# Landmark attention and two MLPs on one core: two PSUM tiles for attention's banks, SyncE in written order, and a new order of the casts in batch 0

## The chip, the cores and the metric

One core of one Trainium2 chip. The metric is the device time of one execution in microseconds; three runs of the kernel before gave 1353.11, 1353.55 and 1353.95, median 1353.55.

## The reference

All tensors are float32. Batch 8, 8 heads, 576 positions, head size 64, 32 landmarks.

```
A  = softmax(q k_lm^T)      # q_lm, k_lm: means over 18 neighbouring positions
Bm = softmax(q_lm k_lm^T)
C  = softmax(q_lm k^T)
Z  = Bm^T / (norms of Bm);  six times: Z = 2 Z - Z Bm Z
x  = A Z C v                              # 4608 tokens x 512
x  = elu(x w_in) w_out                    # 512 -> 2048 -> 512
out = max(x w1, x w2, x w3) w_out2        # 512 -> 768 -> 512
```

## The kernel before

The program has two phases. The first goes through 256 slots, 32 for each of 8 batches, and makes attention and the first MLP; the second makes the maxout MLP from a copy of x in DRAM. The change is in the first phase only, almost all of it in batch 0's slots.

**A slot** (loop at L1414) is one half of a batch's tokens (288) and one block of 128 of the 2048 hidden features. `h_mm` (L689) issues six matmuls into `ph` (PSUM, two buffers) and on ScalarE Relu and Exp into `eh` (SBUF, two buffers); `h_post` (L706) finishes elu on VectorE (the post, L708) and splits the result into a rounded part `gt`, a cast on ScalarE (L97), and the low rest of it, a subtraction on GpSimd or VectorE (L99). In batch 0 that split is made one slot late; `G_LOW` says in which slots VectorE makes the subtraction. `x_mm` (L718) issues twelve matmuls of the slot three back, from `gt` and `wo`, into `x`. In batch 0 the features go in two passes (slots 0 to 7 and 8 to 15 are the two halves of the tokens with the first 8 blocks, 16 to 31 the rest); at the end of each pass ScalarE and VectorE copy `x` out, or VectorE adds it to what an earlier pass left.

**Attention's output is never multiplied out.** `w_step` (L656) multiplies the small matrix `mt` of a batch with 512 columns of w_in, in a pair of PSUM banks, and splits the result into `wp`, the weights of `h_mm`: a cast on ScalarE (L665) and a subtraction on VectorE (L670), the latter issued late in the slot. `w_both(n)` is that for batch 0 and n = 1 to 3.

**Weights** w_in and w_out arrive as 64-bit words (512 KB an item, 32 items) and are narrowed to float32 on the chip. An item is fetched into a place that an earlier item has left (`fetch1`, L1266, twelve places at most), widened on ScalarE (L114; in the form `BITS` a second ScalarE instruction, L119, scales the low word, in the form `BITS_V` VectorE does so, L127), narrowed on VectorE (L136), and, for w_out, cast (L182, ScalarE) and subtracted (L187, GpSimd). Items 0 to 9 are widened in the front, the part ahead of slot 0; from item 10 on a slot widens one item at its start and narrows, casts and subtracts the ones before it at its end.

**Attention of the next batch** runs inside the slots: `SECOND_SLOTS` gives the slot of each step for batch 1, all behind the post of the slot before (`after_post`). Steps: `q0`..`k1` sum q and k over 18 positions on VectorE (L300); `c0`, `c1` score C (L323: per half a pair of banks, a maximum on VectorE, L351, and a copy on ScalarE, L358, for each); `e`, `t` transpose; `cv` multiplies with v; `bbt` and `n0` to `n5` are Newton's steps (L612: a matmul, a product on VectorE, L580, a copy on ScalarE, L631, an add on VectorE, L633); `a10` to `a31` are A's softmax (L426: maximum on VectorE, subtraction on GpSimd, L432; exp on ScalarE, L440); `m` copies `mt` (L653).

**PSUM for attention** is one tile `banks` of two banks; `att_ps` gives out one bank in turn, `att_pair` both. In batch 0's front the banks of the MLP are used instead (tiles `pc`, `pe`, `pn`, `pa`, `pw` and so on).

**Order.** TensorE and VectorE run in the order written, ScalarE too until slot 27. In the front a string, `ORDER`, sets the order of attention's steps (letters B, V, A), of narrowings (c) and of widenings (w). SyncE, which issues all DMAs, and GpSimd are ordered by the framework's planner, which lets a DMA go ahead of one written earlier. Each queue is in order once it is planned: an instruction that waits holds all behind it. The framework makes an instruction wait for the earlier ones on the tiles that it touches.

```
banks = ps_a.tile([P, 2, 512], F32, name="banks")
...
turn[0] ^= 1
return Bank(banks[:, turn[0]], turn[0])
```

Of the kernel before, what the change touches and what calls it, by code (L numbers as in the profile page):

```python
# [9 lines left out]
F32 = mybir.dt.float32  # L10
# [9 lines left out]
def landmark_attention_mlp_maxout_kernel(  # L20
# [13 lines left out]
    nc = tc.nc  # L34
# [16 lines left out]
    FPN = 512 // P  # L51
    LAG = 3

    FIXED_ACT = 27
    RA = 3

    AHEAD2 = 5
# [2 lines left out]

    NF = 12
    DEPTH = 12
    EARLY = {2: range(8, 22), 3: range(8, 26)}
    FRONT = 10
    BY_ACT = range(12, 17)
    PAIRS = "i0 i0 o0 i1 i1 o2 o4 o6 i2 i2 o8 i3 i3 o10 o12 o14".split()

    ORDER = "BBBBwwBBVBBVVVVwwBVVBAcwBAwBcAwBAAwBAAwBAwBAAWc"


    G_LOW = [[0, 1] * 8, [0, 1] * 8]
# [74 lines left out]
    class Conversions:  # L146
# [58 lines left out]

    manual = ExitStack()
    manual.enter_context(
        tc.manual_schedule(engines={mybir.EngineType.DVE, mybir.EngineType.Activation})
    )

    ident = const.tile([P, P], F32, name="ident")
# [22 lines left out]

    spare = [0]

    banks = ps_a.tile([P, 2, 512], F32, name="banks")
    turn, last = [0], [None, None]

    class Bank:  # L240
# [19 lines left out]
    def att_ps(b, name):  # L260

        if b == 0 and spare[0] >= 0:
            spare[0] += 1
            n = spare[0] % 6
            if n < 4:
                return Bank(ps_x.tile([P, 512], F32, tag=f"x{n}", name=name))
            return Bank(ps_h.tile([P, 512], F32, tag="h", name=name))
        turn[0] ^= 1
        return Bank(banks[:, turn[0]], turn[0])

    def att_pair(b, name):

        if b == 0 and spare[0] >= 0:
            return [att_ps(b, name) for _ in range(2)]
        return [Bank(banks[:, g], g) for g in range(2)]

    def load_qk(b, r, nm):

# [147 lines left out]
    def soft_a1(b, g):  # L426
        x = state["x", b, g]
        sh = [P, 2 * NB2, M]
        t = att.tile([P, 2 * NB2], F32, tag=f"t18{g}", name="t18")
        nc.vector.tensor_reduce(out=t, in_=x, op=ALU.max, axis=AX.X)  # L430
        eng = nc.gpsimd if b < 2 and SOFT_SUB[b][g] else nc.vector
        eng.tensor_tensor(  # L432
            out=x, in0=x, in1=t.unsqueeze(2).to_broadcast(sh), op=ALU.subtract
        )
        if b:
            soft_ax(b, g)

    def soft_ax(b, g):
# [173 lines left out]
    def newton(b, i):  # L612
        cur, nxt, rd = rrs[i % 2], rrs[(i + 1) % 2], state.pop(("rd", b))
        pvs = []
        for gs in groups(b):
            pt = att_ps(b, "pn")
            pv = pt[:, : 2 * P].rearrange("p (g c) -> p g c", g=2)
            for g in gs:
                pt.put(
                    nc.tensor.matmul,  # L620
                    pv[:, g],
                    rd[:, g].rearrange("p h m -> p (h m)"),
                    cur[:, g],
                    start=True,
                    stop=True,
                )
# [5 lines left out]
        for gs, sl, pv in pvs:
            nc.vector.tensor_tensor(  # L633
                out=nxt[:, sl, M : M + D],
                in0=pv[:, sl, M : M + D],
                in1=cur[:, sl, M : M + D],
                op=ALU.add,
            )
# [50 lines left out]
    def h_mm(b, half, f):  # L689
        n, ff = divmod(f, FPN)  # L690
        ph = ps_h.tile([P, 512], F32, tag="h", name="ph")
        for g in range(2):
            wt = state["wp", b, n, g]
            wh = wt[:, 0, ff * P : (ff + 1) * P]
            wl = wt[:, 1, ff * P : (ff + 1) * P]
            ah, al = state["ah", b, half][:, g], state["al", b, half][:, g]
            for j, (a, c) in enumerate(((wh, ah), (wh, al), (wl, ah))):
                nc.tensor.matmul(  # L698
                    ph[:, :HF], a, c, start=(g == 0 and j == 0), stop=(g == 1 and j == 2)
                )  # L700
        e = r_s.tile([P, HF], F32, tag="eh", name="eh", bufs=2)
        nc.scalar.activation(e, ph[:, :HF], AF.Relu, scale=-1.0)  # L702
        nc.scalar.activation(e, e, AF.Exp, scale=-1.0)  # L703
        hps[b, half, f] = (ph, e)

    def h_post(b, half, f):  # L706
        ph, e = hps.pop((b, half, f))
        state["post"] = nc.vector.scalar_tensor_tensor(  # L708
            out=e, in0=e, scalar=1.0, in1=ph[:, :HF], op0=ALU.subtract, op1=ALU.max
        )  # L710
        held.append(((b, half, f), e))
        while len(held) > (b == 0):
# [478 lines left out]
    def att_steps(b):  # L1191
# [172 lines left out]
    def after_post(stp):  # L1364


        def go():
            with tc.issue_after(state["post"].ins):
                stp()

        return go

    at(0, load_att, 1)
    at(2, load_v, 1)
    for b in range(1, B):
        t0 = (b - 1) * NSL
        if b > 1:
# [36 lines left out]
    for t, sl in enumerate(seq):  # L1414
        if t == 0:
            scalar.close()
            scalar = ExitStack()
            manual.enter_context(tc.manual_schedule(engines={mybir.EngineType.PE}))
            vector.enter_context(tc.manual_schedule(engines={mybir.EngineType.DVE}))
            scalar.enter_context(tc.manual_schedule(engines={mybir.EngineType.Activation}))  # L1420
        if t == FIXED_ACT:
            scalar.close()
        h_mm(*sl)
        if t < len(items):
            stage(conv.widen, FRONT + t, form(FRONT + t))
        late = [fn(*args) for fn, args in plan[t]]
        h_post(*sl)
        for fn in late:
# [143 lines left out]
```

## Time and profile before

| | us |
|---|---|
| median of three runs | 1353.55 |
| profiled execution | 1353.35 |
| its span, first to last instruction | 1351.1 |
| front, up to the first matmul of slot 0 | 41.8 |
| slots 0 to 27 | 108.9 |
| mean granted TensorE clock, share of full speed | 0.987 |

The span is what the trace covers; 2.25 us of the profiled execution lie outside it. Busy times of engines overlap and don't add up. A row of a timeline merges neighbouring instructions of one kind: start, time from its start to the last one's end, engine, line, operation, output and inputs, count, and in brackets the idle time of the engine just before and what ended it.

### The profile page before, as it was taken

Reading aid. Unit: us, or ns where it says so; the run is one execution under the profiler, and the core shown is the slowest. Engines: PE = TensorE matmul, PEld = TensorE weight load, DVE = VectorE, ACT = ScalarE, POOL = GpSimd, SP = SyncE. Lnnn points to the kernel's source line nnn. Section 1 sums busy time; section 2 is a strip of 40 time slices with the busy share of each in tenths; the row PEclk is TensorE's granted clock in tenths of the full one; section 3 lists DMA queues with packets and bytes.
Section 4 is the critical chain, followed back from the end, with each engine's and each line's share of the span. In section 5 each row is a group of like instructions: output and inputs, shape, how many; then the busy total and the mean of one; then the engine's idle time right before and its main releaser. Section 6 shows DMA issues by size and latency. Waiting matters only on the chain.

```text
span 1351.1 us, 28435 instructions
## 1 busy us (share of the span) xinstructions
PE 1300.8 (96%) x11144; PEld 1228.5 (91%) x11144; DVE 834.0 (62%) x1613; ACT 672.2 (50%) x1559; POOL 656.9 (49%) x675
## 2 busy tenths in 40 slices
PE   4688999999999999999999999999999999999998
PEld 2577889899898998998999999999999999999998
DVE  7876745546546546455464456776677667668873
ACT  4665555656656656656566652322223223236451
POOL 1423323534435425435356456666666666665443
PEclk8789999999999999999999999999999999999999
DMA  9644105214214232242116243221322132279872
GB/s 354 231 127 156 36 19 166 73 68 135 100 56 136 92 120 90 66 166 85 56 66 189 65 132 98 87 98 55 114 87 87 56 110 91 86 281 324 295 243 79
DMA packets 102374, 168.03 MB, mean 124 GB/s; under 512 B 5984, under 2 KB 57824, under 8 KB 102240
## 3 DMA queue, kind: packets, MB, share of 16 engines
q1 hardware_dynamic: 102240, 166.22, 36.3%
q8 instruction: 87, 1.43, 0.4%
q14 instruction: 47, 0.39, 0.1%
HBM read 107.22 MB, written 58.98 MB: 123 GB/s over the span
## 4 chain that ended last, share of the span: by engine, by line
PE 85%; ACT 1%; DVE 1%; issue 1%; POOL 1%; DMA 0%; SPq 0%; DVEq 0%; POOLq 0%; ACTq 0%
PE p L1087 30%; PE x L733 27%; PE ph L698 13%; PE p L1164 10%; PE banks L256 6%; DMA words<-in_moe_w_dram 0%; POOL gt L99 0%; ACT eh L703 0%; ACT eh L702 0%; ACT wp L665 0%; DVE wp L670 0%; DVE eh L708 0%; DVE kT L300 0%; ACT gt L97 0%; POOL al L99 0%
## 5 line engine op out<-in xcount | busy, mean ns | idle before, releaser
L733 PE MATMUL x<-gt,wo 128*128 128x288 f32 x3072 | 471.5, 303 | 4.3 <-DVE xo L757 2.0
L733 PEld LDWEIGHTS x<-gt,wo 128*128 128x128 f32 x3072 | 425.2, 190 | 47.0 <-issue 27.7
L1087 PE MATMUL p<-xo,w 128*128 128x256 f32 x3402 | 410.3, 283 | 1.0 <-DVE xo L761 1.0
L1087 PEld LDWEIGHTS p<-xo,w 128*128 128x128 f32 x3402 | 408.6, 191 | 2.8 <-ACT xo L903 1.5
L99 POOL TENSOR_TENSOR gt<-eh,gt 128x288 fp32r<-128x288 f32 x240 | 195.7, 817 | 356.7 <-ACT gt L97 306.2
L698 PE MATMUL ph<-ah,wp 128*128 128x288 f32 x1024 | 250.4, 299 | 3.3 <-DVE eh L708 2.4
L708 DVE SCALAR_TENSOR_TENSOR eh<-eh,ph 128x288 f32<-128x288 f32 x256 | 114.4, 447 | 163.9 <-ACT eh L703 120.3
L942 POOL TENSOR_TENSOR u<-s,v 128x512 f32<-128x512 f32 x99 | 132.4, 1337 | 145.7 <-DVE v L940 144.1
L698 PEld LDWEIGHTS ph<-ah,wp 128*128 128x128 f32 x1024 | 181.8, 192 | 8.5 <-DVE eh L708 4.0
L702 ACT ACTIVATE eh<-ph 128x288 f32<-128x288 f32 x256 | 105.0, 410 | 124.2 <-PE ph L698 92.7
L97 ACT CAST gt<-eh 128x288 fp32r<-128x288 f32 x256 | 110.0, 430 | 103.4 <-DVE eh L708 103.4
L931 ACT COPY s<-p 128x512 f32<-128x512 f32 x99 | 58.0, 586 | 199.4 <-PE p L1087 166.5
L698 PE MATMUL ph<-al,wp 128*128 128x288 f32 x512 | 153.3, 299 | 0.0
L1164 PE MATMUL p<-wo,ho 128*128 128x256 f32 x1134 | 133.2, 280 | 0.0
L1164 PEld LDWEIGHTS p<-wo,ho 128*128 128x128 f32 x1134 | 133.1, 188 | 0.0
L703 ACT ACTIVATE eh<-eh 128x288 f32<-128x288 f32 x256 | 114.1, 446 | 5.6
L955 DVE TENSOR_TENSOR t<-p,u 128x512 f32<-128x512 f32 x81 | 55.7, 688 | 72.1 <-POOL u L942 69.6
L698 PEld LDWEIGHTS ph<-al,wp 128*128 128x128 f32 x512 | 98.0, 191 | 0.0
L1154 DVE TENSOR_TENSOR ho<-hf,ho 128x768 fp32r<-128x768 f32 x54 | 73.4, 1387 | 13.8 <-ACT ho L1152 13.1
L1094 DVE TENSOR_TENSOR t<-t 128x1024 f32<-128x1024 f32 x54 | 70.7, 1308 | 6.4 <-POOL t L945 0.4
L945 POOL TENSOR_TENSOR t<-u,s 128x256 f32<-128x256 f32 x81 | 67.2, 829 | 5.4
L1152 ACT CAST ho<-hf 128x768 fp32r<-128x768 f32 x63 | 51.1, 836 | 36.5 <-DMA hf<-hs 17.3
(165 smaller groups left out, 1342.2 us busy)
## 6 DMA issues: line engine op xcount, KB each, us to landing
hf<-hs SPq DMA_DIRECT2D x63, 384.0 KB, 4.4
hs<-t SPq DMA_DIRECT2D x27, 512.0 KB, 3.0
xs<-xo SPq DMA_DIRECT2D x36, 288.0 KB, 4.2
hs<-s SPq DMA_DIRECT2D x27, 384.0 KB, 3.4
qT<-in_q_dram SPq DMA_DIRECT2D x16, 576.0 KB, 6.1
kT<-in_k_dram SPq DMA_DIRECT2D x16, 576.0 KB, 7.6
words<-in_moe_w_dram SPq DMA_DIRECT2D x9, 1024.0 KB, 5.6
xf<-xs SPq DMA_DIRECT2D x9, 1024.0 KB, 5.1
```

The lines of the kernel that those rows point to most:

```text
L97: nc.scalar.copy(hi, src)
L99: eng.tensor_tensor(out=lo, in0=src, in1=hi.bitcast(F32), op=ALU.subtract)
L256: ins = fn(*args, **kw)
L698: nc.tensor.matmul(ph[:, :HF], a, c, start=(g == 0 and j == 0), stop=(g == 1 and j == 2))
L702: nc.scalar.activation(e, ph[:, :HF], AF.Relu, scale=-1.0)
L703: nc.scalar.activation(e, e, AF.Exp, scale=-1.0)
L708: state["post"] = nc.vector.scalar_tensor_tensor(out=e, in0=e, scalar=1.0, in1=ph[:, :HF], op0=ALU.subtract, op1=ALU.max)
L733: nc.tensor.matmul(xacc[ec][:, :HF], a, gt[:, c], start=(first and j == 0), stop=(last and j == 2),)
L942: nc.gpsimd.tensor_tensor(out=u57, in0=s57, in1=v.unsqueeze(1).to_broadcast([P, 2, 256]), op=ALU.add)
L1087: nc.tensor.matmul(dst, l, r, start=(c == 0 and j == 0), stop=(c == 1 and j == 2))
L1154: eng.tensor_tensor(out=lo, in0=v, in1=hi.bitcast(F32), op=ALU.subtract)
L1164: nc.tensor.matmul(dst, l, r, start=(c == 0 and n == 0), stop=(c == NP - 1 and n == 2))
```

## The change

Seven things change. (1) `banks` becomes two tiles of one bank each. (2) SyncE joins the engines in written order, up to slot 14. With it the loads of batch 1's q and k are written in slots 1 and 2 and that of v in slot 5. (3) In batch 0 the cast of `gt` of slot t-1 follows Exp of slot t on ScalarE, and its subtraction stands ahead of the post of slot t; `G_LOW` is turned round. (4) Widening moves from the start to the end of a slot, and all stages of an item from 10 on stand a slot later. (5) `BY_ACT` is empty: items 12 to 16 take the form in which VectorE scales the low word. `EARLY` gives the places of `wp` for one item less. (6) For batch 1 the exp of A's softmax is a step of its own (`ax0`, `ax1`), a slot behind its subtraction at the earliest, the sums stand a slot later, and Newton's add is issued behind the post. (7) `w_both(1)` moves from slot 2 to 3, `w_both(3)` from 17 to 18.

```
-    FIXED_ACT = 27
+    FIXED_SP, FIXED_ACT = 14, 27
-    EARLY = {2: range(8, 22), 3: range(8, 26)}
+    EARLY = {2: range(8, 21), 3: range(8, 26)}
-    BY_ACT = range(12, 17)
+    BY_ACT = ()
-    G_LOW = [[0, 1] * 8, [0, 1] * 8]
+    G_LOW = [[1, 0] * 8, [1, 0] * 8]
...
-        tc.manual_schedule(engines={mybir.EngineType.DVE, mybir.EngineType.Activation})
+        tc.manual_schedule(
+            engines={mybir.EngineType.DVE, mybir.EngineType.Activation, mybir.EngineType.SP}
+        )
...
-    banks = ps_a.tile([P, 2, 512], F32, name="banks")
+    banks = [ps_a.tile([P, 512], F32, tag=f"bank{g}", name=f"bank{g}") for g in range(2)]
...
-        return Bank(banks[:, turn[0]], turn[0])
+        return Bank(banks[turn[0]], turn[0])
...
-        return [Bank(banks[:, g], g) for g in range(2)]
+        return [Bank(banks[g], g) for g in range(2)]
...
-        if b:
+        if b > 1:
             soft_ax(b, g)
...  newton: the adds become a function add
+        if b == 1:
+            return add
+        add()
...
         nc.scalar.activation(e, e, AF.Exp, scale=-1.0)
         hps[b, half, f] = (ph, e)
+        gt_cast()
 
     def h_post(b, half, f):
         ph, e = hps.pop((b, half, f))
+        gt_low()
...
         held.append(((b, half, f), e))
-        while len(held) > (b == 0):
-            key, e = held.pop(0)
-            gt = r_s.tile([P, 2, HF], F32R, tag="gt", name="gt", bufs=LAG + 1)
-            split(e, gt[:, 0], gt[:, 1], key[0] == 0 and G_LOW[key[1]][key[2]])
-            gts[key] = gt
+        if b:
+            gt_cast()
+            gt_low()
+
+    def gt_cast():
+
+        for key, e in held:
+            gts[key] = gt = r_s.tile([P, 2, HF], F32R, tag="gt", name="gt", bufs=LAG + 1)
+            nc.scalar.copy(gt[:, 0], e)
+
+    def gt_low():
+        for (b, half, f), e in held:
+            gt = gts[b, half, f]
+            eng = nc.vector if b == 0 and G_LOW[half][f] else nc.gpsimd
+            eng.tensor_tensor(
+                out=gt[:, 1], in0=e, in1=gt[:, 0].bitcast(F32), op=ALU.subtract
+            )
+        held.clear()
...
+        if b == 1:
+            first += [(f"ax{g}", lambda g=g: soft_ax(b, g)) for g in range(2)]
...  SECOND_SLOTS
-        q0=3, k0=4, q1=5, k1=6, ...
+        q0=4, k0=5, q1=6, k1=7, ...
-        a10=20, a11=21, a20=23, ...
+        a10=20, a11=21, ax0=21, ax1=22, a20=23, ...
...
-    at(0, load_att, 1)
-    at(2, load_v, 1)
+    for n, (g, nm) in enumerate(((0, "q"), (0, "k"), (1, "q"), (1, "k"))):
+        at(1 + n // 2, load_qk, 1, g, nm)
+    at(5, load_v, 1)
...
-        at(tw - (2 if n == 1 else 3), w_both, n)
+        at(tw - (1, 3, 2)[n - 1], w_both, n)
...
+        if t == FIXED_SP:
+            sync.close()
...
         h_mm(*sl)
-        if t < len(items):
-            stage(conv.widen, FRONT + t, form(FRONT + t))
...
-        if t < len(items):
-            stage(conv.narrow, FRONT + t - 1, form(FRONT + t - 1))
-            stage(conv.cast, FRONT + t - 2)
-            stage(conv.low, FRONT + t - 2)
+        it = FRONT + t - 1
+        if it < len(items) + 2:
+            stage(conv.narrow, it - 1, form(it - 1))
+            stage(conv.cast, it - 2)
+            stage(conv.low, it - 2)
+            stage(conv.widen, it, form(it))
```

## Rows read from the trace of the kernel before

**Rows 1.** The page: busy times of all engines, and the group of the posts.

```profile
PE 1300.8 (96%) x11144; PEld 1228.5 (91%) x11144; DVE 834.0 (62%) x1613; ACT 672.2 (50%) x1559; POOL 656.9 (49%) x675
...
L708 DVE SCALAR_TENSOR_TENSOR eh<-eh,ph 128x288 f32<-128x288 f32 x256 | 114.4, 447 | 163.9 <-ACT eh L703 120.3
```

**Rows 2.** Table by stage: stretch, us, busy PE PEld DVE ACT POOL, clock, DMA share, GB/s.

```profile
0.00:41.80 41.80, 17.77 (x203) 10.21 (x203) 30.26 (x91) 21.42 (x52) 6.56 (x12) 0.82 0.94 346
41.80:55.00 13.20, 10.34 (x53) 8.37 (x54) 10.02 (x16) 8.92 (x20) 5.15 (x4) 0.66 0.76 263
55.00:86.50 31.50, 24.71 (x179) 21.86 (x178) 24.74 (x50) 24.23 (x55) 12.33 (x11) 0.92 0.50 145
86.50:99.20 12.70, 10.89 (x116) 9.34 (x116) 10.87 (x30) 7.85 (x17) 3.94 (x4) 0.93 0.22 81
99.20:113.80 14.60, 13.82 (x155) 11.63 (x154) 9.20 (x23) 8.74 (x20) 1.60 (x2) 1.00 0.46 154
113.80:150.70 36.90, 29.67 (x225) 26.61 (x224) 25.11 (x56) 20.82 (x52) 17.60 (x17) 0.95 0.34 105
180.00:1310.00 1130.00, 1128.32 (x9669) 1080.08 (x9662) 691.83 (x1302) 554.68 (x1293) 591.03 (x609) 1.00 0.35 118
```

**Rows 3.** Chain in order of time, 200 to 250 us: one undisturbed slot.

```profile
230.95 0.80 PE ph L698 x6
231.75 1.61 PE x L733 x12
```

**Rows 4.** Waits of TensorE from 42 us on: us in total, times, longest.

```profile
PE banks L256 <- DVE rr L633: 5.2, 5, 3.9
PE banks L256 <- DVE w_in_sb L136: 2.8, 1, 2.8
PE banks L256 <- ACT e L358: 2.1, 1, 2.1
```

**Rows 5.** Timeline of the front: SyncE, ScalarE and VectorE.

```profile
21.09 0.38 SPq L288 DMA_DIRECT2D v<-in_v_dram  x1
...
34.90 0.66 ACT L114 ACTIVATE w_in_sb<-words 128x512 f32<-128x512 f32 x1 [1.83 <-DMA words<-in_moe_w_in_dram]
...
36.91 0.78 DVE L457 STREAM_TRANSPOSE af<-x 128x576 f32<-128x576 f32 x1
37.69 0.66 ACT L114 ACTIVATE w_in_sb<-words 128x512 f32<-128x512 f32 x1 [1.57 <-DMA words<-in_moe_w_in_dram]
...
38.94 1.43 ACT L97 CAST ah<-af 128x288 fp32r<-128x288 f32 x4
```

**Rows 6.** Timeline of slots 4 and 5: VectorE and GpSimd.

```profile
56.71 1.34 DVE L300 TENSOR_REDUCE qs<-qT 128x64 f32<-128x1152 f32 x1
...
58.21 1.28 POOL L187 TENSOR_TENSOR wo<-wf,wo 128x512 fp32r<-128x512 f32 x1
...
58.34 1.70 DVE L136 SCALAR_TENSOR_TENSOR wf<-wf,words 128x512 uint32<-128x512 uint32 x1
```

**Rows 7.** Instructions on tile words to 110 us: count, shortest/median/longest ns, first, last.

```profile
L119 ACT ACTIVATE words<-words x15: 639/662/692, 11.3 to 67.0; 128x512 uint32<-128x512 uint32 x15
...
L127 DVE TENSOR_SCALAR words<-words x11: 412/422/1017, 49.8 to 105.8; 128x512 uint32<-128x512 uint32 x11
L136 DVE SCALAR_TENSOR_TENSOR wf<-wf,words x10: 680/693/1773, 43.0 to 91.3; 128x512 uint32<-128x512 uint32 x10
```

**Rows 8.** Waits over the whole span: Relu of a slot on GpSimd.

```profile
ACT eh L702 <- POOL gt L99: 25.2, 31, 2.1
```

**Rows 9.** Timeline of slot 8's scores: first copy, second maximum.

```profile
72.86 0.38 ACT L358 COPY e<-banks 128x288 f32<-128x288 f32 x1
73.27 0.46 DVE L351 TENSOR_REDUCE mx<-banks 128x1 f32<-128x288 f32 x1 [2.09 <-ACT e L358]
```

**Rows 10.** Timeline of Newton's third step in batch 1: widening, then the matmul.

```profile
127.10 0.66 ACT L114 ACTIVATE wf<-words 128x512 f32<-128x512 f32 x1 [1.51 <-POOL wo L187]
...
128.24 0.71 PE L256 MATMUL banks<-rr,rd 128*128 128x128 f32 x4 [3.88 <-DVE rr L633]
```

More of the change, by code (lines that the diff above doesn't have):

```diff
@@ L631, in newton, with add @@
                 nc.scalar.copy(nxt[:, sl, :M], pv[:, sl, :M])
[L632 to L638, printed above, removed]
+        def add():
+            for gs, sl, pv in pvs:
+                nc.vector.tensor_tensor(
+                    out=nxt[:, sl, M : M + D],
+                    in0=pv[:, sl, M : M + D],
+                    in1=cur[:, sl, M : M + D],
+                    op=ALU.add,
+                )
+        if b == 1:
+            return add
+        add()
     def m_step(b):
@@ L711, in h_post @@
         held.append(((b, half, f), e))
-        while len(held) > (b == 0):
-            key, e = held.pop(0)
-            gt = r_s.tile([P, 2, HF], F32R, tag="gt", name="gt", bufs=LAG + 1)
-            split(e, gt[:, 0], gt[:, 1], key[0] == 0 and G_LOW[key[1]][key[2]])
-            gts[key] = gt
+        if b:
[11 more added lines that the diff above has]
+                out=gt[:, 1], in0=e, in1=gt[:, 0].bitcast(F32), op=ALU.subtract
+            )
+        held.clear()
     def x_mm(b, half, f):
@@ L1227, in landmark_attention_mlp_maxout_kernel @@
     SECOND_SLOTS = dict(
-        q0=3, k0=4, q1=5, k1=6, c0=8, c1=9, c20=11, c21=11, e0=12, b=10, b2=11, cv0=14, e1=15,
+        q0=4, k0=5, q1=6, k1=7, c0=8, c1=9, c20=11, c21=11, e0=12, b=10, b2=11, cv0=14, e1=15,
         nb=13, ah0=16, cv1=17, bbt=18, ah1=19, t0=13, t1=16, n0=20, n1=21, n2=22, n3=23, n4=24, n5=25, m=26,
-        a10=20, a11=21, a20=23, a21=24, a30=25, a31=26,
+        a10=20, a11=21, ax0=21, ax1=22, a20=23, a21=24, a30=25, a31=26,
     )
@@ L1368, in go @@
             with tc.issue_after(state["post"].ins):
-                stp()
+                return stp()
         return go
-    at(0, load_att, 1)
-    at(2, load_v, 1)
+    for n, (g, nm) in enumerate(((0, "q"), (0, "k"), (1, "q"), (1, "k"))):
+        at(1 + n // 2, load_qk, 1, g, nm)
+    at(5, load_v, 1)
     for b in range(1, B):
@@ L1404, in landmark_attention_mlp_maxout_kernel @@
     scalar, manual = manual, ExitStack()
-    vector = ExitStack()
+    vector, sync = ExitStack(), ExitStack()
     def form(k):
@@ L1420, in landmark_attention_mlp_maxout_kernel @@
             scalar.enter_context(tc.manual_schedule(engines={mybir.EngineType.Activation}))
+            sync.enter_context(tc.manual_schedule(engines={mybir.EngineType.SP}))
+        if t == FIXED_SP:
+            sync.close()
         if t == FIXED_ACT:
```

## The prediction

> **What bounds the kernel now.** I read four views in this order. The page's busy line says TensorE is busy 96% of the span [rows 1], so any gain must come from the few per cent left. The table by stage says where those are: from 180 to 1310 us PE is busy 1128.3 of 1130.0 us at a granted clock of 1.00, while the stages before 150.7 us are holed and partly at a lower clock, 0.66 in slots 0 to 3 [rows 2]. (A stage begins with the first `ph` matmul of a slot: slot 0 at 41.8, slot 4 at 55.0, 12 at 86.5, 15 at 99.2, 19 at 113.8, 28 at 150.7.) A slot that nothing disturbs is 0.80 us of `ph` and 1.61 us of `x` matmuls, 2.41 us [rows 3]; the first 28 slots take 108.9 us, 3.9 each. The waits of PE name what it lacks there: results of VectorE and ScalarE [rows 4]. So the kernel is bound by TensorE from slot 28 on, and before that by the chain ScalarE, VectorE, GpSimd of batch 0 and of batch 1's attention. Whatever ends slot 28 earlier ends the kernel earlier: behind it PE has no idle time to swallow a gain.
>
> **The change, part by part.**
>
> *SyncE in written order (the front).* Before, the loads of batch 1's q, k and v (four of 0.59 MB, v 1.18 MB, 3.5 MB in all) went out inside the front; v at 21.09 [rows 5]. At the front's 346 GB/s [rows 2] they fill the queues for 10.2 us. ScalarE widens the ninth and tenth weight item only after waiting 1.83 and 1.57 us for their words, and the copy of `mt`, on which the first `pw` matmuls hang, is queued behind them on ScalarE [rows 5]. Written order puts those loads into slots 1, 2 and 5, so both waits (3.40 us) should go. Next late is `af`: its second transpose ends at 36.91 + 0.78 = 37.69. ScalarE's third cast of `ah` ran at 38.94 + 2 x 0.36 = 39.66 and can now run at 37.69, 1.97 us earlier; VectorE's `al` and `wp` stand behind it. I take -2.0; ends 0 (another transfer is late) and -3.4. What the new order costs: the fetch of item 12 waits until item 4 is narrowed, which on VectorE comes behind the first two low parts of `wp`, three instructions of about 0.69 after slot 0 starts, 39.8 + 2.1 = 41.9; items 13 to 17 and all of q and k queue behind it. Six words of 0.52 MB, q and k of 1.18 MB make 4.3 MB, 12.5 us at 346 GB/s: the first q and k land at about 54, the second pair, behind items 18 and 19, near 61. VectorE's first sum on them, in slot 4 from now on, will want its q at about 55.0 - 3.0 = 52 (by this part and the next), the fourth three slots of some 3 us later, near 61. I allow up to 2 us there, inside the part on slots 4 to 11.
>
> *Slots 0 to 3: `w_both(1)` one slot later, no widening in slot 0.* PE stands 2.8 us for the narrowing of items 8 and 9 [rows 4], with slot 3's six `ph` matmuls unissued (0.80 at full clock, 0.80 / 0.66 = 1.2 here). Now these go first and fill 1.2 us of it, and the pair itself is wanted later. Against it, VectorE's `gt_low` of slot 0 (put at the 0.45 of a post, the same shape [rows 1]) stands ahead of that narrowing. I take -1.0; ends -2.8 and +0.8.
>
> *`BY_ACT` empty.* Five items lose a ScalarE scaling of 0.66 us (L119) and give VectorE one of 0.42 us (L127) [rows 7]. Slots 4 to 7 hold four of them, beside the four sums of 1.34 [rows 6], just where VectorE has least room. So +4 x 0.46 (with the gap to the next) = +1.8 of VectorE time on the path; ends 0 and 4 x 1.02 = +4.1, the longest L127 in the trace.
>
> *`gt`'s cast behind exp, and two tiles for two banks (slots 4 to 11, 31.5 us).* In batch 0 Relu of slot t waits until the low part of slot t-2 is made, since `eh` has two buffers: 25.2 us in 31 waits on GpSimd alone [rows 8]. Its cast stood behind a widening (0.66, with L119 1.32); now it stands behind exp, so the low part starts that much earlier and ScalarE no longer trails PE by a slot. At the pairs of `score_c` the one tile shows: the second `mx` reads bank 1, yet waited 2.09 us for the copy of bank 0 [rows 9]; PE then waited 2.1 us [rows 4]. With two tiles the two maxima follow each other (2 x 0.46). What is late next is VectorE: it was busy 24.7 of these 31.5 us [rows 2], and 1.8 come from L127: 26.5. PE's own need is less: 24.7 busy at 0.92 of the clock, 22.7. I take VectorE's load and 0.5 us at its ends: 27.0, a gain of 4.5 net of L127. Ends: +1.8 (L127 and nothing freed) and -7.0 (two L136 without a stretch of 1.0 as in [rows 6]).
>
> *Slots 12 to 14 (12.7 us).* PE is busy 10.9 at 0.93 of the clock, a need of 10.1 [rows 2]. The wait of a pair on `exp_t2`'s copy stays, since a pair needs both banks; `wp`'s low parts start half a microsecond earlier (bank 0's no longer waits for bank 1's cast). I take -1.0; ends 0 and -2.6. *Slots 15 to 18 (14.6):* PE 13.8 busy, the third `w_both` only moves by a slot: 0; ends -0.8 and +1.0.
>
> *Widening last, `soft_ax` a slot later, Newton's add behind the post (slots 19 to 27, 36.9 us).* The longest wait of PE is here, 3.9 us [rows 4]: ScalarE's widening waited 1.51 for GpSimd's `wo`, Newton's copy was queued behind it and the next matmul started at 128.24 [rows 10]. The exp of `x` held the same queue for GpSimd's subtraction. Each cause moves off: the widening behind the copy, the exp a slot behind its subtraction. The add now lets one post pass, 0.45 [rows 1]; the slot's `x` and the next `ph` matmuls, 2.41 us, hide that, so I cost it at nothing; where VectorE is behind by more than that cover, it costs 0.45 in each of five slots. PE is busy 29.7 at 0.95 of the clock, a need of 28.2. VectorE's 25.1 is 2.8 a slot [rows 2], but the slots of `a11` and `a20` hold another 128x576 instruction of about 0.78 [rows 5], some 3.6 each, 1.2 above 2.41. So 28.2 + 2 x 1.2 = 30.6, a gain of 6.3; ends -8.7 and -2.0 (the one longest wait halved).
>
> *The port of VectorE and GpSimd.* The row first: L136 takes 0.69 us, but 1.70 at 58.34, beside a GpSimd subtraction from 58.21 [rows 6]; longest 1.77, and L127 0.42 to 1.02 [rows 7]. My sums keep today's mix of short and long. The Trainium skill, page "SBUF — State Buffer", section "Who interferes with whom", says that a VectorE instruction with two SBUF inputs, or one in a two-port mode, and a GpSimd instruction that reads SBUF lock each other out for a whole instruction. By that rule, taken to its end, the added L127 and the low parts moved next to them would each lose a GpSimd instruction; the sum would then be that of the second rival below.
>
> Sum: 2.0 + 1.0 + 4.5 + 1.0 + 0 + 6.3 = 14.8 us. The profiled execution took 1353.35 (span 1351.1 and 2.25 around it), so 1338.55; it was 0.2 below the median of 1353.55, so 1338.7.
>
> **The rivals.**
> 1. *All of it comes:* the far ends, 3.4 + 2.8 + 7.0 + 2.6 + 0.8 + 8.7 = 25.3 us, some 1328. For: each wait has a named cause. Against: VectorE is already 79% busy in slots 4 to 11. Chance 0.06.
> 2. *VectorE becomes the bound through the shared port:* four L127 at 1.02 for 0.46 add 2.2, and ten more narrowings at 1.70 for 0.69, half of them on the path, 5.0: 14.8 - 7.2 = 7.6, about 1346. For: [rows 6]. Against: the median L136 is 0.69 [rows 7]. Chance 0.19. The Trainium skill's page "SBUF — State Buffer" would have it so, were GpSimd always there first.
> 3. *Two tiles change nothing,* the same engines' order holding the banks apart: the 2.1 us at the pairs stay, and about 1 us of `wp`: 1341.8. Against: [rows 9], where the banks differ. Chance 0.08.
> 4. *Slower: batch 1's q and k come late.* VectorE works in order; a sum without its data holds the post, and with it PE. Place: slots 4 to 7. If the loads ran at the 145 GB/s of today's slots 4 to 11 [rows 2] rather than 346, 4.3 MB take 30 us and the second 2.2 MB another 15: the last k lands at 87, the fourth sum wants it at 61, 26 us lost against 14.8 gained: 1365. It decides from a landing at 76 on. For: the loads leave the front, and a SyncE queue in order cannot step past a word that waits. Against: 145 GB/s is what was asked for there, not what the queues can do. Chance 0.07.
>
> **How the numbers follow.** The forecast (14.8 us, its own range 1331.5 to 1344.5) has 0.60. With rivals 1 to 3 that is 0.93 for a gain of some size; I take 0.06 of rival 2 as a gain too small to be told (0.2% is 2.7 us, about what a measurement of this kernel can tell from no change). Faster 0.87, same 0.06, slower 0.07. Low end 1331, high end 1347, which takes in rival 3 and most of rival 2.
>
> **What would show it.** Slot 0's first `ph` matmul near 39.8 and no ScalarE wait for words before it; the second `mx` right behind the first; no Relu waiting a microsecond for GpSimd in slots 4 to 8; Newton's gap of 3.9 us gone; slot 28 near 136. I am wrong if slot 4 to slot 12 takes over 30 us with VectorE full (rival 2), if a sum waits for a q or k load (rival 4), or if slot 28 comes early and PE idles behind it.

## The result, and the profile after

Four runs of the changed kernel gave 1335.39 to 1337.04 us, median 1336.07; the kernel before, on the same chip, 1353.75. The ratio is 0.9866, 95% interval [0.9849, 0.9883], a gain of 17.7 us. The profiled execution took 1336.0 us with a span of 1334.2.

The busy line of the page, against [rows 1]: TensorE's busy time is 5 us less (the clock, last section), VectorE's 5 us more.

```profile
PE 1295.7 (97%) x11144; PEld 1223.3 (92%) x11144; DVE 839.3 (63%) x1618; ACT 671.4 (50%) x1554; POOL 657.2 (49%) x675
```

The table by stage, columns as in [rows 2], cut at the same slots (0, 4, 12, 15, 19, 28):

```profile
0.00:39.20 39.20, 17.68 (x202) 10.17 (x202) 29.64 (x91) 21.35 (x52) 6.34 (x12) 0.84 0.74 265
39.20:52.03 12.83, 10.28 (x52) 7.53 (x53) 11.82 (x18) 8.67 (x20) 4.26 (x4) 0.69 0.72 234
52.03:78.19 26.16, 22.34 (x178) 19.81 (x177) 24.40 (x48) 20.61 (x49) 11.35 (x10) 1.00 0.92 325
78.19:90.21 12.02, 11.11 (x118) 8.72 (x116) 11.50 (x33) 7.84 (x17) 2.81 (x4) 1.00 0.42 134
90.21:105.16 14.95, 13.77 (x156) 11.65 (x155) 9.98 (x23) 8.43 (x19) 4.17 (x4) 1.00 0.49 150
105.16:135.36 30.20, 27.73 (x224) 25.07 (x223) 29.72 (x60) 21.91 (x55) 18.20 (x16) 1.00 0.44 139
163.10:1293.00 1129.90, 1128.90 (x9684) 1080.76 (x9683) 691.74 (x1302) 557.92 (x1294) 591.37 (x609) 1.00 0.35 118
```

Slot 28 begins 15.3 us earlier (150.7 to 135.4): 2.6 in the front, 0.4 in slots 0 to 3, 5.3 in 4 to 11, 0.7 in 12 to 14, -0.35 in 15 to 18, 6.7 in 19 to 27. Now look at the third column of busy times, VectorE's: 24.4 of 26.2 us in slots 4 to 11 and 29.7 of 30.2 in slots 19 to 27. So it looks like the bound of both, which [rows 2] did not show; u_byact, g_pool and best2 below test that. The gain in these two stages is VectorE's idle time. Its waits there, by the view of [rows 4]: before in slots 4 to 11, then changed; at last before in slots 19 to 27, where the changed kernel has none:

```profile
DVE mx L351 <- ACT e L358: 2.6, 2, 2.1
DVE eh L708 <- ACT eh L703: 2.6, 2, 2.1
DVE gt L99 <- ACT gt L97: 1.2, 3, 0.5
...
DVE eh L718 <- ACT eh L711: 1.1, 1, 1.1
...
DVE rr L633 <- ACT rr L631: 6.0, 5, 2.0
DVE gt L99 <- ACT gt L97: 2.6, 2, 1.9
DVE eh L708 <- ACT eh L703: 2.4, 1, 2.4
```

In slots 4 to 11 waits for ScalarE fall from 6.4 to 1.1 us, for a gain of 5.3. In slots 19 to 27 they fall from 11.0 to none, while VectorE's busy time rises by 4.6, for a gain of 6.7. Of the 4.6, some 1.1 is one more item (L127, L136) and 1.4 two more low parts of `wp`; the rest, by this estimate about 2 us, is instructions that took longer beside GpSimd (second rival, below).

Waits of TensorE from 39 us on, columns as in [rows 4]:

```profile
PE ph L706 <- DVE eh L718: 3.9, 3, 2.5
PE bank L258 <- DVE rr L637: 2.5, 3, 1.0
PE ph L706 <- ACT wp L673: 1.6, 1, 1.6
...
PE bank L258 <- ACT e L360: 1.2, 1, 1.2
```

Newton's longest wait fell from 3.9 to 1.0 us, and the 2.8 us on the narrowing of w_in are gone. New at the top is the post: 2.5 us at one place, where the first matmul of slot 3 waits for the post of slot 1. The timeline around it (VectorE, GpSimd, then TensorE):

```profile
42.58 2.38 DVE L136 SCALAR_TENSOR_TENSOR w_in_sb<-w_in_sb,words 128x512 uint32<-128x512 uint32 x2
42.76 3.31 POOL L187 TENSOR_TENSOR wo<-wf,wo 128x512 fp32r<-128x512 f32 x2 [4.25 <-ACT wo L182]
...
44.88 1.51 DVE L736 TENSOR_TENSOR gt<-eh,gt 128x288 fp32r<-128x288 f32 x1
...
46.81 0.40 PE L706 MATMUL ph<-ah,wp 128*128 128x288 f32 x1 [2.53 <-DVE eh L718]
```

Two narrowings (2.38 where two take 1.38) and the low part of slot 0 (1.51 where it takes 0.45) run beside two subtractions of GpSimd, and the post stands behind them.

The front, against [rows 5]: both widenings run without a wait for words, `mt` is copied 3.4 us earlier (38.79 before), the third cast of `ah` waits for nothing but `af`, and the first matmul of slot 0 now waits for the cast of `wp`.

```profile
33.14 0.66 ACT L114 ACTIVATE w_in_sb<-words 128x512 f32<-128x512 f32 x1
...
34.25 0.66 ACT L114 ACTIVATE w_in_sb<-words 128x512 f32<-128x512 f32 x1
...
35.37 0.25 ACT L661 COPY mt<-pm 128x128 f32<-128x128 f32 x1
...
37.90 0.76 ACT L97 CAST ah<-af 128x288 fp32r<-128x288 f32 x2 [0.69 <-DVE af L459]
...
39.20 0.61 PE L706 MATMUL ph<-ah,wp 128*128 128x288 f32 x1 [1.57 <-ACT wp L673]
```

The scores of slot 8, against [rows 9]: the two maxima are one row of 0.81 us, with no wait between them. And the first sum on batch 1's q, in slot 4:

```profile
54.40 1.35 DVE L302 TENSOR_REDUCE qs<-qT 128x64 f32<-128x1152 f32 x1 [0.15 <-DMA qT<-in_q_dram]
...
67.95 0.81 DVE L353 TENSOR_REDUCE mx<-bank 128x1 f32<-128x288 f32 x2
...
69.25 0.77 PE L258 MATMUL bank<-kT,qs 64*32 64x320 f32 x16 [1.17 <-ACT e L360]
```

### The profile page after: what moved, and what is told of

Same layout as the page of the kernel before. It is cut to its first block, busy times and chain, and to the rows that moved or that the text cites. A ratio compares the mean times of both kernels' runs of the same rounds, so it can differ in the third digit from the quotient of the medians.

```text
span 1334.2 us, 28407 instructions
## 1 busy us (share of the span) xinstructions
PE 1295.7 (97%) x11144; PEld 1223.3 (92%) x11144; DVE 839.3 (63%) x1618; ACT 671.4 (50%) x1554; POOL 657.2 (49%) x675
## 3 DMA queue, kind: packets, MB, share of 16 engines
q8 instruction: 87, 1.43, 0.4%
## 4 chain that ended last, share of the span: by engine, by line
PE 91%; DVE 5%; ACT 1%; DMA 1%; issue 1%; SPq 0%; POOL 0%; DVEq 0%; ACTq 0%
PE p L1110 31%; PE x L756 29%; PE ph L706 14%; PE p L1187 10%; PE bank L258 7%; DMA qT<-in_q_dram 1%; DMA kT<-in_k_dram 1%; DVE w_in_sb L136 1%; DVE words L127 1%; DVE wf L136 1%; DVE eh L718 0%; DVE gt L736 0%; DVE kT L302 0%; DVE wp L678 0%; DVE rr L637 0%
## 5 line engine op out<-in xcount | busy, mean ns | idle before, releaser
L718 DVE SCALAR_TENSOR_TENSOR eh<-eh,ph 128x288 f32<-128x288 f32 x256 | 114.4, 447 | 171.4 <-ACT eh L711 138.8
L1175 ACT CAST ho<-hf 128x768 fp32r<-128x768 f32 x63 | 51.2, 836 | 36.9 <-DMA hf<-hs 17.6
```

Source lines behind the costliest of these rows:

```text
L718: state["post"] = nc.vector.scalar_tensor_tensor(out=e, in0=e, scalar=1.0, in1=ph[:, :HF], op0=ALU.subtract, op1=ALU.max)
```

## The experiments

A name with u undoes one part of the changed kernel, one with a adds one part to the kernel before. Stages in us, from the first `ph` matmul of a slot to that of another; ratio with its interval against the kernel before on the same chip.

| | front | 0-3 | 4-11 | 12-14 | 15-18 | 19-27 | slot 28 | ratio |
|---|---|---|---|---|---|---|---|---|
| before | 41.8 | 13.2 | 31.5 | 12.7 | 14.6 | 36.9 | 150.7 | 1 |
| changed | 39.2 | 12.8 | 26.2 | 12.0 | 15.0 | 30.2 | 135.4 | 0.9866 [0.9849, 0.9883] |
| u_tile | 39.5 | 13.5 | 28.3 | 11.5 | 14.9 | 30.7 | 138.4 | 0.9898 [0.9885, 0.9912] |
| u_sync | 43.0 | 12.8 | 26.4 | 12.0 | 14.9 | 30.2 | 139.3 | 0.9888 [0.9875, 0.9901] |
| u_cast | 39.1 | 12.9 | 29.3 | 12.7 | 15.4 | 35.3 | 144.7 | 0.9927 [0.9914, 0.9940] |
| u_widen | 39.6 | 13.6 | 26.2 | 12.0 | 15.0 | 32.0 | 138.4 | 0.9880 [0.9866, 0.9895] |
| u_soft | 39.3 | 12.9 | 26.2 | 12.0 | 14.9 | 33.5 | 138.8 | 0.9893 [0.9880, 0.9907] |
| u_byact | 39.0 | 12.8 | 24.8 | 12.0 | 14.9 | 30.2 | 133.7 | 0.9858 [0.9845, 0.9872] |
| low_after | 39.5 | 12.8 | 25.8 | 11.9 | 14.6 | 30.8 | 135.4 | 0.9869 [0.9856, 0.9883] |
| g_pool | 38.8 | 13.6 | 25.1 | 11.3 | 14.7 | 29.3 | 132.8 | 0.9843 [0.9830, 0.9857] |
| a_sync | 40.0 | 13.2 | 31.5 | 12.7 | 14.6 | 36.9 | 148.9 | 0.9978 [0.9969, 0.9986] |
| a_cast | 43.3 | 15.1 | 25.9 | 12.7 | 14.8 | 33.2 | 145.0 | 0.9939 [0.9926, 0.9952] |
| best1 | 40.0 | 13.0 | 23.6 | 11.3 | 14.8 | 29.2 | 131.9 | 0.9830 [0.9816, 0.9843] |
| best2 | 39.3 | 13.0 | 23.6 | 11.3 | 14.7 | 28.0 | 129.9 | 0.9826 [0.9813, 0.9840] |

Each row but the ratio is one profiled execution. Where an edit cannot touch it, the front still scatters by up to 0.8 us and slots 0 to 3 by as much (the clock, last section). Not undone singly: the moves of `w_both`, the sums and the stages of an item a slot later, and the turn of `G_LOW`; what these are worth is not shown.

**u_tile: one tile for the two banks.**

```
-    banks = [ps_a.tile([P, 512], F32, tag=f"bank{g}", name=f"bank{g}") for g in range(2)]
+    banks = ps_a.tile([P, 2, 512], F32, name="banks")
-        return Bank(banks[turn[0]], turn[0])
+        return Bank(banks[:, turn[0]], turn[0])
-        return [Bank(banks[g], g) for g in range(2)]
+        return [Bank(banks[:, g], g) for g in range(2)]
```

> The changed kernel, with attention's two banks again one tile; nothing else. Theory (the one tile makes a pair's second maximum wait for the first bank's copy): at the scores of slots 8 and 9 the second maximum starts about 2 us behind the first, as in [rows 9], where it now follows directly, TensorE waits about 2 us there, and the low parts of wp start half a microsecond later; in all 2 to 4 us over the changed kernel, about 1339. Rival (third rival of the prediction, the tiles change nothing since the order of the engines holds the banks apart anyway): within 0.8 us of the changed kernel, about 1336.

Its timeline at slot 8's scores: VectorE's second maximum waits for ScalarE's copy of the other bank again, and TensorE waits 1.72 where it waited 1.17.

```profile
68.97 0.45 DVE L353 TENSOR_REDUCE mx<-banks 128x1 f32<-128x288 f32 x1
...
69.88 0.46 DVE L353 TENSOR_REDUCE mx<-banks 128x1 f32<-128x288 f32 x1 [0.47 <-ACT e L360]
...
70.82 0.77 PE L258 MATMUL banks<-kT,qs 64*32 64x320 f32 x16 [1.72 <-ACT e L360]
```

Slots 4 to 11 grow by 2.1 us, so the third rival (the tiles change nothing) falls. The price at the pair is small (0.47, not the 2.09 of [rows 9]; 0.55 more for TensorE), so the expected 2 us at each were wrong; 0.6 of the 2.1 come in slot 9 and 1.4 in slot 11. This run's low clock in slots 0 to 3 (last section) is not the reason, since u_widen had it too and its slots 4 to 11 did not grow. Slots 12 to 14 do not grow either: over slots 4 to 14 the tiles are worth 1.6 us.

**u_sync: SyncE by the planner, loads in slots 0 and 2.**

```
-            engines={mybir.EngineType.DVE, mybir.EngineType.Activation, mybir.EngineType.SP}
+            engines={mybir.EngineType.DVE, mybir.EngineType.Activation}
-        at(1 + n // 2, load_qk, 1, g, nm)
-    at(5, load_v, 1)
+    at(0, load_att, 1)
+    at(2, load_v, 1)
```

> The changed kernel, with SyncE ordered by the planner again and batch 1's loads written in slots 0 and 2 as before. Theory (the front's 2.6 us came from loads of q, k and v that went out ahead of words): ScalarE waits for words near 34 and 37 us again, the first matmul of slot 0 moves from 39.2 back to about 41.8, and the end from 1336.1 to about 1338.5. Rival 1 (the front was shortened by something else, the order of items or casts): slot 0 stays near 39.2 and the time within 0.8 us. Rival 2 (the written order costs more in slots 4 to 11, where DMA share rose to 0.92, than it gives in the front): slot 0 at 41.8 but slots 4 to 11 shorter than 26.2, and the end at or under 1336.

The waits for words are back, the first longer than in [rows 5] (2.98 for 1.83). ScalarE's timeline in the front:

```profile
36.08 0.67 ACT L114 ACTIVATE w_in_sb<-words 128x512 f32<-128x512 f32 x1 [2.98 <-DMA words<-in_moe_w_in_dram]
...
38.87 0.66 ACT L114 ACTIVATE w_in_sb<-words 128x512 f32<-128x512 f32 x1 [1.57 <-DMA words<-in_moe_w_in_dram]
39.97 0.25 ACT L659 COPY mt<-pm 128x128 f32<-128x128 f32 x1
```

The front grows by 3.8 and every other stage stays within 0.2. So the part is worth 3.8 in the changed kernel, all of it in the front, and the full DMA queues of slots 4 to 11 (325 GB/s against 176 here) cost nothing that shows.

**a_sync: the same part alone, on the kernel before.** The diff of the last one the other way round; the sums stay in slots 3 to 6.

```
+    FIXED_SP, FIXED_ACT = 14, 27
...
+    for n, (g, nm) in enumerate(((0, "q"), (0, "k"), (1, "q"), (1, "k"))):
+        at(1 + n // 2, load_qk, 1, g, nm)
+    at(5, load_v, 1)
...
+            sync.enter_context(tc.manual_schedule(engines={mybir.EngineType.SP}))
```

> The kernel before, with SyncE alone in written order to slot 14 and batch 1's loads written in slots 1, 2 and 5; the sums on them stay in slots 3 to 6, a slot earlier than in the changed kernel. Theory (the front gains whatever the rest does; the sums are then wanted before their data): slot 0 starts near 39.2 instead of 41.8; in the changed kernel the first q was issued at 45.4 and its sum in slot 4 waited 0.15 us at 54.4, so a sum in slot 3, near 50, waits 3 to 5 us for q and holds the posts; the end between 1351 and 1355. Rival (no wait, the planned order of the other engines hides it): the whole 2.6 us stay, 1351 or less, and no sum waits for a load.

The front gains 1.8 us, no stage behind it changes, and no sum waits for a load: the step written in slot 3 runs behind that slot's post, and VectorE came to it at 55.1. The theory's wait was wrong; of the rival's 2.6 us, 1.8 show in this trace and 3.0 in the ratio (0.0022 x 1355). The same part is worth 1.8 here and 3.8 above because the front under the planner is not one thing: the widening that waits starts at 34.90 before, at 36.08 in u_sync and at 36.36 in a_cast (below), though no edit of u_sync beyond SyncE's own, and none of a_cast, is about the front.

**u_cast: gt's cast at the post instead of behind Exp.**

```
         hps[b, half, f] = (ph, e)
-        gt_cast()
...
         ph, e = hps.pop((b, half, f))
+        gt_cast()
         gt_low()
```

> The changed kernel, with the cast of batch 0's gt issued at the post (behind whatever the slot's attention has put on ScalarE) instead of right behind Exp; the low part's place stays. Theory (the cast's place is what frees eh early): in slots 4 to 11 Relu waits for the low part come back at a microsecond each, that stage grows from 26.2 by 3 to 5 us, the end is near 1340. Rival (most of slots 4 to 11 came from widening last and from the low part ahead of the post; the cast's place is worth little once no widening stands ahead of it): the end moves by under 1 us.

The largest part of all, 9.3 us at slot 28, and 5.1 of them in slots 19 to 27, for which neither the prediction nor this expectation had a term. Its timeline there shows how: the cast stands behind Newton's copy and the exp of A, VectorE's low part waits for it, the post and Newton's add stand behind the low part, and TensorE waits 2.51 us.

```profile
118.86 0.21 ACT L633 COPY rr<-bank 128x64 f32<-128x64 f32 x1 [1.30 <-DVE rd L582]
118.97 0.69 ACT L442 ACTIVATE x<-x 128x576 f32<-128x576 f32 x1
119.56 0.42 ACT L730 CAST gt<-eh 128x288 fp32r<-128x288 f32 x1
...
120.01 1.05 DVE L736 TENSOR_TENSOR gt<-eh,gt 128x288 fp32r<-128x288 f32 x1 [0.52 <-ACT gt L730]
...
121.78 1.11 PE L258 MATMUL bank<-rr,rd 128*128 128x128 f32 x4 [2.51 <-DVE rr L637]
```

**a_cast: the cast behind Exp, the low part ahead of the post and G_LOW turned round, alone on the kernel before.** The part of the diff that touches `h_mm`, `h_post`, `gt_cast`, `gt_low` and `G_LOW`, cut here:

```
-    G_LOW = [[0, 1] * 8, [0, 1] * 8]
+    G_LOW = [[1, 0] * 8, [1, 0] * 8]
...
         hps[b, half, f] = (ph, e)
+        gt_cast()
...
         ph, e = hps.pop((b, half, f))
+        gt_low()
```

> The kernel before, with part 3 of the change alone: gt's cast behind exp, its low part ahead of the post, G_LOW turned round. Undone in the changed kernel this part cost 9 us (3.1 in slots 4 to 11, 0.7, 0.4, 5.1 in slots 19 to 27). Theory (it works by itself: eh comes free earlier in every slot of batch 0): slots 4 to 11 gain 2 to 4, slots 19 to 27 gain 2 to 5 us, the end 5 to 9 us under the kernel before. Rival (it works only with the widening last, since Relu, Exp and cast still stand behind a widening that waits, and the low part ahead of the post then holds the post): a gain under 2 us, or a loss.

Slots 4 to 11 gain 5.6 and slots 19 to 27 3.7 us, so it works by itself; the rival falls. It gives 3.4 of that back: 1.5 in the front, where its waits for words total 4.3 us, and 1.9 in slots 0 to 3, where TensorE now stands 4.1 us for the narrowing of w_in (2.8 in [rows 4]). In the changed kernel neither wait stands. TensorE's longest wait of this run:

```profile
PE banks L256 <- DVE w_in_sb L136: 4.1, 1, 4.1
```

**u_widen: widening at the slot's start.**

```
         h_mm(*sl)
+        it = FRONT + t - 1
+        if it < len(items) + 2:
+            stage(conv.widen, it, form(it))
...
-            stage(conv.widen, it, form(it))
```

> The changed kernel, with the widening of the same item issued at the slot's start, behind the six matmuls, instead of last in the slot. Theory (a widening that waits for its words or for GpSimd holds ScalarE's copies and exps behind it): waits of ScalarE on words or on wo come back ahead of Newton's copies, slots 19 to 27 grow from 30.2 by 3 to 6 us and slots 4 to 11 by 1 to 2; the end near 1341. Rival (slots 19 to 27 were shortened by the exp a slot later and Newton's add behind the post, not by the widening): slots 19 to 27 stay within 1 us, the end within 1 us of 1336.

Widening waits 3.7 us for GpSimd again (its row among ScalarE's waits, 39 to 145 us), but slots 19 to 27 grow by 1.8 only, and slots 4 to 11 not at all. A miss by half.

```profile
ACT wf L114 <- POOL wo L187: 3.7, 3, 2.1
```

**u_soft: exp with its subtraction, Newton's add at once.**

```
-        if b == 1:
-            return add
         add()
...
-        if b > 1:
+        if b:
             soft_ax(b, g)
```

> The changed kernel, with the exp of A's softmax again in the same step as its subtraction and Newton's add again right behind its copy; sums and scores stay where they are. Slots 19 to 27 took 36.9 us before and 30.2 us changed; with the cast late they took 35.3, with the widening first 32.0. Theory (prediction: exp stands in front of Newton's copies and waits for GpSimd's subtraction of 1.2 to 1.4 us, twice): slots 19 to 27 grow by 2.5 to 4.5 us, the end near 1340. Rival (cast and widening already account for 5.1 + 1.8 = 6.9 of the 6.7 us, so this part is worth nothing): slots 19 to 27 within 0.8 us of 30.2, the end within 1 us of 1336.

Slots 19 to 27 take 33.5, 3.3 more. Its timeline: the exp waits for GpSimd's subtraction twice, with Newton's copies behind it.

```profile
113.59 0.69 ACT L442 ACTIVATE x<-x 128x576 f32<-128x576 f32 x1 [2.73 <-POOL x L434]
...
118.95 0.69 ACT L442 ACTIVATE x<-x 128x576 f32<-128x576 f32 x1 [2.40 <-POOL x L434]
...
122.29 0.72 PE L258 MATMUL bank<-rr,rd 128*128 128x128 f32 x4 [2.26 <-DVE rr L637]
```

The rival's arithmetic was wrong: undone one by one, cast, widening and exp cost 5.1 + 1.8 + 3.3 = 10.2 us in a stage that gained 6.7. They are links of one chain, Relu, Exp, cast, copy, and whichever is late holds the rest; such costs don't add.

**u_byact: items 12 to 16 scaled on ScalarE.**

```
-    BY_ACT = ()
+    BY_ACT = range(12, 17)
```

> The changed kernel, with items 12 to 16 scaled on ScalarE (0.66 us each) again instead of on VectorE (0.42 us). Theory (VectorE is the bound of slots 4 to 11, busy 24.4 of 26.2 us, while ScalarE is busy 20.6): four or five instructions with 0.46 each off VectorE, slots 4 to 11 take 24.4 to 25.4, the end 1 to 2 us under the changed kernel, 1334 to 1335. Rival (the chain through ScalarE, Relu, Exp, cast, sets the slot, and VectorE's L127 lies beside it): slots 4 to 11 grow by 0.5 to 2 us.

Slots 4 to 11 fall to 24.8 us and VectorE's busy time there from 24.4 to 22.7, while ScalarE's rises from 20.6 to 22.9 at no cost that shows. So VectorE's load sets the time of this stage. The ratio alone would not tell it (0.0008 under the changed kernel's, inside its interval). Its table by stage, slots 4 to 11:

```profile
51.80:76.60 24.80, 22.17 (x179) 19.85 (x178) 22.71 (x42) 22.85 (x54) 10.90 (x10) 1.00 0.95 345
```

**low_after: the low part behind the post.**

```
         ph, e = hps.pop((b, half, f))
-        gt_low()
...
+        gt_low()
         held.append(((b, half, f), e))
```

> The changed kernel, with the low part of gt of slot t-1 behind the post of slot t on VectorE and GpSimd instead of ahead of it. Theory (ahead of the post it holds TensorE: slot 1's low part took 1.51 us beside GpSimd's 3.31 us and the next slot's first matmul then waited 2.53 for the post): that wait falls under 1.5 us, slots 0 to 3 take 11.8 instead of 12.8, the other stages within 0.5, the end near 1335. Rival (Relu of slot t+1 waits for the low part of slot t-1, since eh has two buffers; each slot on VectorE pays the post's 0.45): slots 4 to 27 grow by 2 to 4 us, the end near 1339.

Neither. The wait for the post falls to 0.8, but slots 0 to 3 stay at 12.8: a wait for the narrowing of w_in takes its place (TensorE's waits of this run):

```profile
PE ph L706 <- DVE eh L717: 1.5, 2, 0.8
...
PE bank L258 <- DVE w_in_sb L136: 1.2, 1, 1.2
```

The same VectorE work stands there in another order. The low part's place is worth nothing that this run can tell; how many of the low parts VectorE makes at all is what counts, as the next run shows for slots 4 to 14 and 19 to 27.

**g_pool: all low parts of gt in batch 0 on GpSimd.**

```
-    G_LOW = [[1, 0] * 8, [1, 0] * 8]
+    G_LOW = [[0] * 16, [0] * 16]
```

> The changed kernel, with all of batch 0's low parts of gt on GpSimd (0.8 us each) and none on VectorE (0.44, some 1.16). Theory (VectorE's load sets slots 4 to 11 and 19 to 27, GpSimd is busy 11.4 of 26.2 and 18.2 of 30.2 us): four or five instructions less on VectorE in each stage, slots 4 to 11 shorter by 1 to 2 us, slots 19 to 27 by 0.5 to 1.5, the end near 1334. Rival (GpSimd's own order: a low part waits behind a subtraction of wo of 1.3 us, eh comes free later and Relu waits about a microsecond for GpSimd in these slots): both stages grow, together by 2 to 5 us, the end near 1339.

Slots 4 to 11 lose 1.1, 12 to 14 0.7, 19 to 27 0.9 us, though GpSimd is busy 22.4 of 29.3 us there. The rival's waits are there (Relu waits 1.9 us for GpSimd in slots 4 to 27, 1.1 at most), but they cost less than VectorE's relief gives. Slots 0 to 3 take 0.8 more, which is within that stage's scatter (clock 0.63, changed 0.69), so it is not shown that VectorE should keep any low part there, as the next kernels have it.

**best1 and best2: both ways together.** The diff of best2; best1 has `BY_ACT = range(12, 17)`.

```
-    BY_ACT = ()
+    BY_ACT = (12, 13, 14, 15, 16, 28, 29, 30, 31)
-    G_LOW = [[1, 0] * 8, [1, 0] * 8]
+    G_LOW = [[1, 0, 1] + [0] * 13, [0] * 16]
```

> The changed kernel, with VectorE relieved in two ways that each helped: items 12 to 16 scaled on ScalarE, and from slot 3 on the low parts of gt all on GpSimd (VectorE keeps those of slots 0 and 2, since slots 0 to 3 grew by 0.8 us without them). Theory (both lift the same load, VectorE's, in different slots): the gains add in part, slots 4 to 11 near 24.0, slots 19 to 27 near 29.3, the end near 1332.5, 2 to 3.5 us under the changed kernel. Rival (with VectorE relieved, ScalarE or GpSimd sets the slot, the gains don't add): within 0.8 us of the kernel with the low parts on GpSimd, 2 us under the changed kernel.

> The kernel of the run before it in this call, with items 28 to 31 (widened in slots 19 to 22) scaled on ScalarE as well. Theory (VectorE sets slots 19 to 27, busy 29.7 of 30.2 us): four instructions of 0.46 off VectorE, another 0.8 to 1.8 us there. Rival (ScalarE's copies of Newton's steps queue behind four more instructions of 0.66 us): slots 19 to 27 grow by up to 2 us.

The table by stage of best2, slots 4 to 11 and 19 to 27:

```profile
52.30:75.90 23.60, 21.59 (x179) 19.74 (x178) 21.58 (x39) 22.45 (x54) 13.53 (x14) 1.00 0.96 350
...
101.90:129.90 28.00, 27.21 (x224) 24.91 (x223) 25.04 (x51) 23.64 (x59) 21.91 (x22) 1.00 0.48 150
```

In slots 4 to 11 the two gains add (1.4 + 1.1 = 2.5, measured 2.6); four more items on ScalarE take 1.2 us off slots 19 to 27. best2 took 1331.36 us, ratio 0.9826 [0.9813, 0.9840], its interval under the changed kernel's: faster than both kernels. TensorE is busy 27.2 of 28.0 us there now, so little is left in that stage.

## Why the prediction was right, and where its steps were not

The time and the direction were right: 1338.7 with a range of 1331 to 1347, measured 1336.07. The sum to slot 28 was 14.8, the trace says 15.3. What is behind slot 28 took 1.6 us less than before, and no step spoke of it. Half a microsecond of that comes with the tiles: in slot 35 TensorE waits 1.19 us for VectorE's add of `x` in all four traces with one tile and 0.72 in all ten with two. In the changed kernel's trace ScalarE makes the first cast of `wp` there ahead of that of `gt`, and VectorE reaches that add sooner (before, then changed):

```profile
173.34 2.10 PE L733 MATMUL x<-gt,wo 128*128 128x288 f32 x12 [1.19 <-DVE xo L757]
...
157.55 2.09 PE L756 MATMUL x<-gt,wo 128*128 128x288 f32 x12 [0.72 <-DVE xo L780]
```

The remaining 1.1 us can be scatter: this part lies between 1198.7 and 1202.2 us in the fourteen traces.

- *Front, 2.0 forecast, 2.6 measured.* Right in mechanism: both waits for words gone, `mt` no longer queued behind them, and `af` next, the third cast of `ah` at 37.90 (forecast 37.69). The rest of the 2.6 is that the cast of `wp` no longer waits for the `pw` matmuls (0.79 before). The size depends on what the planner would have done, 1.8 to 3.8.
- *Loads of q and k.* Forecast: the first lands near 54 and may cost up to 2 us. VectorE waited 0.15 at 54.40, and for no load of batch 1 later. The fourth rival had its price from 145 GB/s; the queues moved 325.
- *Slots 0 to 3, 1.0 forecast, 0.4 measured,* the latter inside that stage's scatter. Mis-sized: the low part of slot 0 was put at 0.45 and took 1.51, and the two narrowings ahead of it took 2.38 instead of 1.38, both beside GpSimd. The end of +0.8 was there for this and the value taken was too hopeful. `w_both(1)` was not moved back alone, so its own share is not shown. Moving the low part did not win it back (low_after).
- *`BY_ACT`, +1.8 forecast.* u_byact puts it at 1.4: the sign right, the size a little high.
- *Slots 4 to 11, 27.0 forecast, 26.2 measured.* Right in the bound: VectorE's load is what was left (24.4 busy against 26.5 counted), and taking load off it shortens the stage. But [rows 8] was misread: its 25.2 us in 31 waits are those of the whole span. In slots 4 to 11 Relu waited 2.3 us for GpSimd, 0.9 at most; 16.1 us, in 21 waits, lie behind slot 28. What the stage lost were VectorE's own waits for ScalarE (the result). So the sign "no Relu waiting a microsecond for GpSimd in slots 4 to 8" told nothing, since the longest before was 0.6; changed, Relu waits 1.2 us there twice, for VectorE's low part. The two causes are shown singly: two tiles 2.1 here (1.6 to slot 14), the cast 3.1 undone and 5.6 alone.
- *Slots 12 to 14, 11.7 forecast, 12.0 measured.* The size held; the reason (with one tile `wp`'s low parts start later) did not show here, since with one tile the stage took 11.5. It stands at 12.7 whenever the cast is late and also with the cast alone; what else it needs stays open.
- *Slots 15 to 18.* 14.6 forecast, 15.0 measured, inside its ends.
- *Slots 19 to 27, 30.6 forecast, 30.2 measured, partly for the wrong reason.* The step said that widening and exp hold Newton's copies. They do (1.8 and 3.3), but it gave the cast nothing in this stage, and the cast is the largest (5.1 undone, 3.7 alone, there with the low part's new place and `G_LOW`). It also counted TensorE's need, 28.2 and 2 x 1.2, while VectorE's load turned out to be the bound: 29.7 us, which the 25.1 of [rows 2] did not promise. That the two sums lie 0.4 us apart is luck.
- *Second rival, the shared port.* The stretches are real. In the timeline of the changed kernel's slots 4 and 6 VectorE's instruction ends 0.3 us behind GpSimd's, and takes 1.43 and 1.17 us where 0.42 and 0.45 are usual:

```profile
51.94 1.29 POOL L187 TENSOR_TENSOR wo<-wf,wo 128x512 fp32r<-128x512 f32 x1 [3.32 <-ACT wo L182]
...
52.09 1.43 DVE L127 TENSOR_SCALAR words<-words 128x512 uint32<-128x512 uint32 x1
...
58.12 1.30 POOL L187 TENSOR_TENSOR wo<-wf,wo 128x512 fp32r<-128x512 f32 x1 [1.74 <-ACT wo L182]
58.56 1.17 DVE L736 TENSOR_TENSOR gt<-eh,gt 128x288 fp32r<-128x288 f32 x1
```

  The rule of the Trainium skill's page "SBUF — State Buffer", section "Who interferes with whom" (a whole instruction is locked out), agrees with these rows within 0.15 us (locked out whole, VectorE's two would end 0.42 and 0.45 behind GpSimd's); that L127, with its one input, runs in a two-port mode no row shows. VectorE's busy time in slots 4 to 11 was 24.4 us (48 instructions) against 24.7 before (50), new L127 included, so the 7.2 us of that rival did not come there. Part of them came in slots 19 to 27: L136 took 0.90 us on average (0.69 before), L127 0.65 (0.58) and the product of A's softmax, L455, 1.12 (0.74), the long ones all beside a GpSimd instruction; that is the estimate of 2 us in the section on the result. Even so, giving GpSimd more to do (g_pool) made the stages shorter.

## What to carry to other kernels

Where three engines pass one buffer round, ask first what stands in each queue ahead of the instruction that frees it: one cast moved ahead was worth more than any transfer or tile here. Undo parts one by one and also add one alone; the costs of links of one chain don't add, and where a wait is removed, other work of the same engine may take its place and leave the time as it was. A transfer order left to a planner makes a stage move by a microsecond or two with edits that have nothing to do with it.

## What was not expected of the hardware

The clock in slots 0 to 3 differs between programs that hardly differ there. u_tile was granted 0.54 of full speed, nearly all of it at the lower of the two levels (1.2 GHz), where the changed kernel got 0.69, and the stage took 13.5 us instead of 12.8; u_widen got 0.53 and 13.6. From 32 to 44 us the clock was at 0.50 or 0.51 in all three; between 44 and 48 us the changed kernel's was at 0.91, that of the other two still at 0.50. What decides it wasn't tried. The row of u_tile in the table by stage:

```profile
39.50:53.00 13.50, 11.19 (x52) 8.33 (x53) 11.67 (x19) 9.02 (x20) 4.59 (x4) 0.54 0.72 239
```

From slot 4 on the changed kernel's clock is 1.00, where [rows 2] show 0.92 and 0.93 in slots 4 to 14 and 0.95 in slots 19 to 27. TensorE had fewer idle stretches and kept the higher level (2.4 GHz); that the one is the reason for the other was not tried. Its busy time in slots 4 to 11 fell from 24.7 to 22.3 us for the same matmuls. Since VectorE's load sets the time of that stage (u_byact), I take this for a consequence of the gain and not a term of it; no run tells the two apart.
